# Which operand stands still: turning the down products of a fused attention and gated MLP kernel

## The chip, the cores and the metric

The kernel runs on one core of a Trainium2 chip. The metric is the device time of one execution in microseconds (us); less is better. The profile is of one execution, taken by the hardware profiler; times inside it count from the start of its span. Engines: PE is TensorE (PEld its weight loads), DVE is VectorE, ACT is ScalarE, POOL is GpSimd, SP is SyncE. A matmul has a stationary operand of 128 x 128, which is loaded first, and a moving operand, of which one column after another passes through.

## The reference

```python
def _attn_ref(r, k, v, w, u):          # B, H, S, D = 4, 8, 768, 48
    state = np.zeros((B, H, D, D))
    for t in range(S):
        cur = np.einsum('bhd,bhe->bhde', u[None] * kt, vt)
        y[:, :, t] = np.einsum('bhd,bhde->bhe', rt, state + cur)
        state = wt[:, :, :, None] * state + np.einsum('bhd,bhe->bhde', kt, vt)

def _moe_ref(x, w_gate, w_val, w_out): # x: 3072 x 384, d_ff = 1536
    gate = 1.0 / (1.0 + np.exp(-(x @ w_gate)))
    val = x @ w_val
    return (gate * val @ w_out)

# reference: y of the attention as rows of 8 * 48 = 384, then the MLP on them
```

## The kernel before

The sequence of 768 tokens is cut into six chunks of 128 (`C`). A chunk of one batch is a place `q = n * 4 + b`: `n` is the chunk, called a row here, `b` the batch. So there are six rows of four places, and a row has 512 tokens.

The attention of a place is a series of small steps (`turn_k`, `sums`, `scores`, `mix`, `turn_x` on PE; `mask`, `take_y` and others on DVE; `bonus1` to `bonus4` on POOL and DVE). They take their PSUM banks from `att_bank`, which hands out two banks in turn. Their result is `x`, the input of the MLP, with the features on the partitions.

The MLP works through `d_ff` in twelve blocks of 128, `f` = 0 to 11. Numbers are kept in two parts, a rounded one (`hi`) and the rest (`lo`), so every product is three matmuls: lo by hi, hi by lo, hi by hi. For one row and one `f`:

- `gate` and `value` each do 9 matmuls (three blocks of 128 features by three parts) into banks `pg` and `pu` (L453). The weights are stationary, the tokens move: 512 columns each.
- `sigmoid` (ACT, L464), `hidden` (DVE, L471), `hidden_hi` (ACT, L475) and `hidden_lo` (DVE, L479) make the two parts `hh` and `hl` of the hidden block, 128 x 512.
- `down` (L488) multiplies them by the output weights: for each of four blocks of 128 tokens, three matmuls in which the block of `hh` or `hl` is stationary and the 384 columns of the weights move. It adds up over `f` in four banks `po0` to `po3`, one per block of tokens. After `f` = 11 it copies each bank to a tile `o` on ACT (L494) and stores that on ACT's queue (L496). `o` comes from a pool with two buffers.

Rows 0 and 1 are done in halves of 256 tokens, in an order worked out at build time by a planner (`Plan`) with costs and due times, while the weights come in and are split (`w_guard` on ACT, `w_body`, `w_sign`, `w_tail`, `w_lo` on DVE, `w_hi` on ACT). Rows 2 to 5 are in an order written out by hand: for every `f`, `gate`, `sigmoid`, a part of the attention of the next row, `value`, the hidden steps, a part, `down` of the block before, a part. Row 5 has no attention beside it. At its first block stands `check_bounds`, a small chain on DVE and PE that sets `flag`.

At the end (L631) every engine loads `flag` and branches past `general`, a slow version of everything that these inputs do not use. Behind the branch the engines meet at a barrier.

```python
for i in range(i0, i1):                                   # down, before
    c = slice((i - i0) * C, (i - i0 + 1) * C)
    for j, (h, w) in enumerate(((hl, whi), (hh, wlo), (hh, whi))):
        nc.tensor.matmul(
            po[n, i][:, :DM], lhsT=h[:, c], rhs=w[f][:, 2 * DM:],
            start=f == 0 and j == 0, stop=f == NFF - 1 and j == 2,
        )
```

The functions that the change touches:

Of the kernel before, what the change touches and what calls it, by code (L numbers as in the profile page):

```python
# [9 lines left out]
F32 = mybir.dt.float32  # L10
F32R = mybir.dt.float32r
BF16 = mybir.dt.bfloat16
# [7 lines left out]
B, H, S, D = 4, 8, 768, 48  # L20
DM, DFF = 384, 1536
P = 128
C = 128
NC_ = S // C
NG = B * NC_
# [4 lines left out]
NFF = DFF // P  # L30
NKT = DM // P
# [13 lines left out]
def general(ctx: ExitStack, tc: tile.TileContext, dec, tok, wts, u, out, whi, wlo, ident):  # L45


    nc = tc.nc
    pool = ctx.enter_context(tc.tile_pool(name="general", bufs=1))
    bank = ctx.enter_context(tc.tile_pool(name="banks", bufs=1, space=PSUM))  # L50
    rows = ctx.enter_context(tc.tile_pool(name="rows", bufs=1, space=bass.MemoryType.DRAM)).tile([B, S, DM], F32, name="rows")

    def tiles(name, shape, dtype=F32):
        return pool.tile(shape, dtype, name=name)

    raw, t, full, square = tiles("raw", [P, HW], mybir.dt.int64), tiles("t", [P, HW], I32), tiles("full", [P, HW]), tiles("square", [P, HW])
    for f in range(NFF):
        for half in range(2):
            cols = slice(half * HW, (half + 1) * HW)
# [19 lines left out]
    vb, y = tiles("vb", [L, B, NP, D]), tiles("yb", [2, B, NP, D])  # L79
# [11 lines left out]
    for c in range(NC_):  # L91
        for b in range(B):
            nc.sync.dma_start(d[:, b], dec[b * NC_ + c])
        with tc.For_i(0, C) as i:
            def at(first, step):
                return d[:, :, first:first + NP * step].rearrange("a b (p c) -> a b p c", c=step)[:, :, :, bass.ds(i, 1)].broadcast_to(shape)
            for o in range(2):
                for b in range(B):
                    nc.sync.dma_start(vb[64 * o:64 * o + D, b], values[c, 2, o, bass.ds(i, 1), b].partition_broadcast(D))
            nc.vector.tensor_tensor(out=kv, in0=vb, in1=at(WW, C), op=ALU.mult)  # L100
            nc.vector.tensor_tensor(out=mix, in0=kv, in1=ub, op=ALU.mult)
            nc.vector.tensor_tensor(out=mix, in0=mix, in1=state, op=ALU.add)
            nc.vector.tensor_tensor(out=mix, in0=mix, in1=at(WW + NP * C, C), op=ALU.mult)
            nc.vector.tensor_tensor(out=state, in0=state, in1=at(1, W1), op=ALU.mult)
            nc.vector.tensor_tensor(out=state, in0=state, in1=kv, op=ALU.add)
            for j in range(2):
                nc.tensor.matmul(py[j][:2, :DM], lhsT=heads, rhs=mix[:, 2 * j:2 * j + 2], start=True, stop=True)
                nc.scalar.copy(y[:, 2 * j:2 * j + 2], py[j][:2, :DM].rearrange("a (b p e) -> a b p e", b=2, e=D))
            for b in range(B):
                for o in range(2):  # L110
                    nc.sync.dma_start(
                        rows[b, bass.ds(c * C + i, 1)].rearrange("t (p o e) -> o t p e", o=2, e=D)[o], y[o:o + 1, b])

    x, px = tiles("x", [P, DM]), bank.tile([P, 512], F32, name="px")
    xhi, xlo = tiles("xh", [P, NKT, C], F32R), tiles("xl", [P, NKT, C], F32R)
    gate, h, hh, hl = tiles("gate", [P, C]), tiles("h", [P, C]), tiles("hh", [P, C], F32R), tiles("hl", [P, C], F32R)
    pg, pu, po = (bank.tile([P, 512], F32, name=n) for n in ("pg", "pu", "po"))
    flat = rows.rearrange("b s e -> (b s) e")
    with tc.For_i(0, NG) as g:
        nc.sync.dma_start(x, flat[bass.ds(g * C, C)])  # L120
        for k in range(NKT):
            nc.tensor.transpose(out=px[:, k * C:(k + 1) * C], in_=x[:, k * P:(k + 1) * P], identity=ident)
        px3 = px[:, :DM].rearrange("a (k c) -> a k c", c=C)
        nc.scalar.copy(xhi, px3)
        nc.vector.tensor_tensor(out=xlo, in0=px3, in1=xhi.bitcast(F32), op=ALU.subtract)
        for f in range(NFF):
            for s, acc in enumerate((pg, pu)):
                for k in range(NKT):
                    cols = slice(s * DM + k * P, s * DM + (k + 1) * P)
                    for j, (w, a) in enumerate(((wlo, xhi), (whi, xlo), (whi, xhi))):  # L130
                        nc.tensor.matmul(acc[:, :C], lhsT=w[f][:, cols], rhs=a[:, k], start=k == 0 and j == 0, stop=k == NKT - 1 and j == 2)
            nc.scalar.activation(gate, pg[:, :C], AF.Sigmoid)
            nc.vector.tensor_tensor(out=h, in0=pu[:, :C], in1=gate, op=ALU.mult)
            nc.scalar.copy(hh, h)
            nc.vector.tensor_tensor(out=hl, in0=h, in1=hh.bitcast(F32), op=ALU.subtract)
            for j, (a, w) in enumerate(((hl, whi), (hh, wlo), (hh, whi))):
                nc.tensor.matmul(po[:, :DM], lhsT=a, rhs=w[f][:, 2 * DM:], start=f == 0 and j == 0, stop=f == NFF - 1 and j == 2)
        nc.scalar.copy(x, po[:, :DM])
        nc.sync.dma_start(out[bass.ds(g * C, C)], x)


class Plan:
# [49 lines left out]
def tile_kernel(ctx: ExitStack, tc: tile.TileContext, dec: bass.AP, tok: bass.AP, wts: bass.AP, u: bass.AP, out: bass.AP):  # L192
    nc = tc.nc
# [3 lines left out]
    p1 = own.enter_context(tc.tile_pool(name="p1", bufs=1))  # L197
    p2 = own.enter_context(tc.tile_pool(name="p2", bufs=2))
    ps1 = own.enter_context(tc.tile_pool(name="ps1", bufs=1, space=PSUM))
    att2 = own.enter_context(tc.tile_pool(name="att2", bufs=2, space=PSUM))  # L200
    early = tc.tile_pool(name="early", bufs=4)
    stage = early.__enter__()

    def att_bank(name):
        return att2.tile([P, 512], F32, tag="att", name=name)

    ident = const.tile([P, P], F32, name="ident")
# [8 lines left out]
    for s in range(2):  # L216
        part = after[s * HC:(s + 1) * HC]
        nc.gpsimd.affine_select(
            out=part, in_=part, pattern=[[1, HC]], compare_op=ALU.is_gt, fill=0.0, base=0, channel_multiplier=-1,
# [14 lines left out]
    raws, fulls, whi, wlo = {}, {}, [None] * NFF, [None] * NFF  # L234
# [5 lines left out]
    def word(f, i, dtype=I32):  # L240
        return raws[f].bitcast(dtype).rearrange("a (c w) -> a c w", w=2)[:, :, i]

    def w_guard(f):
        sq = p1.tile([P, 3 * DM], F32, tag="sq", name=f"sq{f}")
        nc.scalar.activation(sq, word(f, 1, F32), AF.Square, accum_out=acc_s[:, f:f + 1])
        nc.scalar.activation(sq, sq, AF.Relu, bias=1.0, scale=-1.0 / TINY ** 2, accum_out=acc_t[:, f:f + 1])

# [22 lines left out]
    pin, tk, eg, bon, kT, att, ready, mid, bank, x = {}, {}, {}, {}, {}, {}, {}, {}, {}, {}  # L270

    def place(q):
        return q % B * NC_ + q // B
# [183 lines left out]
    po, hid = {}, {}  # L457

    def gate(n, f, i0, i1):
        hid["g", n, f, i0] = up(0, "pg", n, f, i0, i1)  # L460
# [5 lines left out]
    def value(n, f, i0, i1):  # L466
        hid["u", n, f, i0] = up(1, "pu", n, f, i0, i1)
# [13 lines left out]
    def down(n, f, i0, i1):  # L481
        hh, hl = hid["hi", n, f, i0], hid["lo", n, f, i0]
        for i in range(i0, i1):
            if f == 0:
                po[n, i] = ps1.tile([P, 512], F32, tag=f"po{i}", name=f"po{n}_{i}")
# [6 lines that stand above are left out]
            if f == NFF - 1:  # L492
                o = p2.tile([P, DM], F32, tag="o", name=f"o{n}_{i}")
                nc.scalar.copy(o, po[n, i][:, :DM])  # L494
                g = place(n * B + i)
                nc.scalar.dma_start(out[g * C:(g + 1) * C, :], o)  # L496

    def check_bounds():
        nc.vector.tensor_scalar(out=fine[:L, 0], in0=acc_d, scalar1=2.0 ** 90, scalar2=None, op0=ALU.is_le)
# [18 lines left out]
    for q in range(3 * B + 2):  # L518
        k = rank.get(f"c{q}", 99)
# [28 lines left out]
        first = q % B == 0  # L548
# [4 lines left out]
    for f in range(NFF):  # L553
        k = rank[f"w{f}"]
# [7 lines left out]
    for g, (n, i0, i1) in enumerate(GROUPS):  # L562
        m = i1 - i0
        for f in range(NFF):
            a, name = (n, f, i0, i1), f"{g}_{f}"
            k = 100 + f + LAGS[g]
# [15 lines left out]
    plan.run()  # L582
    early.__exit__(None, None, None)
    stage = own.enter_context(tc.tile_pool(name="late", bufs=2))

    def steps(q):

# [20 lines left out]
    last = []  # L608
    nothing = [[lambda: None] * 3] * 3
    for n in range(2, NC_):  # L610
        for j in range(B):
            trio = steps((n + 1) * B + j) if n + 1 < NC_ else nothing
            for i in range(3):
                a = (n, 3 * j + i, 0, B)
                gate(*a)
                sigmoid(*a)
                trio[i][0]()
                value(*a)
                hidden(*a)
                hidden_hi(*a)  # L620
                hidden_lo(*a)
                trio[i][1]()
                if last:
                    down(*last.pop())
                trio[i][2]()
                last.append(a)
                if n == NC_ - 1 and j == 0 and i == 0:
                    check_bounds()
    down(*last.pop())
    own.close()  # L630
    with tc.If(nc.values_load(flag[:1, :1]) != 0):  # L631
        general(tc, dec, tok, wts, u, out, whi, wlo, ident)
# [31 lines left out]
```

## Time and profile before

| | |
|---|---|
| time, median of 3 runs | 614.41 us (611.59 to 615.08) |
| the profiled execution, its own time | 616.97 us |
| its span, first to last instruction | 615.3 us |
| mean granted TensorE clock | 0.980 |
| PE busy | 572.2 us (93%), 6474 matmuls |
| DVE, ACT, POOL busy | 334.5, 201.6, 95.6 us |
| read from and written to HBM | 45.11 and 4.72 MB |

A page of the profile gives each engine's busy time, the span in 40 slices, the DMA queues, the chain of work that ended last and the costliest groups of instructions by line. Further views answer questions on it: groups by line with shapes kept apart, waits, the instructions in order of time, and busy times by stretch. Ends of matmuls are modelled, so the distance from one start to the next tells more than a matmul's own duration.

### The profile page before, as it was taken

What the parts mean: (1) busy time and instruction counts of PE and PEld (TensorE: products, weight loads), DVE (VectorE), ACT (ScalarE), POOL (GpSimd) and SP (SyncE); (2) the same over time, 40 slices, a digit from 0 to 9 for tenths busy, and PEclk for the clock granted to TensorE, in tenths of its full rate; (3) what the DMA queues carried; (4) which work ended last, traced back from release to release, by engine and by line L of the source; (5) the groups of instructions that cost most, each with busy time, mean ns of one, the idle gap of its engine ahead of it and who ended that gap; (6) DMA issues with size and microseconds to landing.
All of it is one profiled execution on the core that took longest, in us unless ns stands there. A gap on an engine that the chain in (4) does not pass through costs nothing. (4 is left out here: it accounts for less than half of the span.)

```text
span 615.3 us, 14604 instructions
## 1 busy us (share of the span) xinstructions
PE 572.2 (93%) x6474; PEld 508.6 (83%) x6474; DVE 334.5 (54%) x570; ACT 201.6 (33%) x402; POOL 95.6 (16%) x86
## 2 busy tenths in 40 slices
PE   4477799999999999799999999999999999999994
PEld 3366699999999999688888888888888888888883
DVE  4989869989675653234544644644544554222220
ACT  2638674434333222312312322312322212221112
POOL 3242011002220503002202202202202200000000
PEclk9998699999999999989999999999999999999998
DMA  8787930032233130121022042022032000000001
GB/s 239 240 330 231 373 111 1 2 85 72 70 128 118 54 122 3 52 84 55 33 85 59 27 136 76 10 84 81 11 131 85 1 1 2 28 26 0 1 2 55
DMA packets 12056, 50.86 MB, mean 83 GB/s; under 512 B 1376, under 2 KB 4576, under 8 KB 10448
## 3 DMA queue, kind: packets, MB, share of 16 engines
q1 hardware_dynamic: 8528, 45.11, 22.7%
q10 hardware_dynamic: 3456, 4.72, 2.2%
q8 instruction: 53, 0.87, 0.6%
q14 instruction: 19, 0.16, 0.1%
HBM read 45.11 MB, written 4.72 MB: 81 GB/s over the span
## 5 line engine op out<-in xcount | busy, mean ns | idle before, releaser
L453 PE MATMUL pg<-x,w 128*128 128x256 f32 (+1 forms) x864 | 174.2, 347 | 1.2 <-DVE w L267 1.2
L453 PE MATMUL pu<-x,w 128*128 128x256 f32 (+1 forms) x864 | 172.1, 345 | 0.0
L453 PEld LDWEIGHTS pg<-x,w 128*128 128x128 f32 x864 | 138.7, 194 | 17.7 <-DVE w L267 1.4
L453 PEld LDWEIGHTS pu<-x,w 128*128 128x128 f32 x864 | 137.6, 193 | 17.4
L488 PE MATMUL po<-w,hh 128*128 128x384 f32 x576 | 148.5, 339 | 0.0
L471 DVE TENSOR_TENSOR sg<-pu,sg 128x256 f32<-128x256 f32 (+1 forms) x96 | 53.4, 557 | 152.8 <-PE pu L453 149.5
L488 PE MATMUL po<-w,hl 128*128 128x384 f32 x288 | 101.9, 354 | 7.1 <-DVE hl L479 6.9
L488 PEld LDWEIGHTS po<-w,hh 128*128 128x128 f32 x576 | 105.8, 190 | 0.9
L475 ACT CAST hh<-sg 128x256 fp32r<-128x256 f32 (+1 forms) x96 | 49.1, 512 | 165.3 <-DVE sg L471 164.8
L464 ACT ACTIVATE sg<-pg 128x256 f32<-128x256 f32 (+1 forms) x96 | 46.9, 488 | 159.9 <-PE pg L453 159.0
L314 POOL TENSOR_TENSOR bon<-tok,a 128x384 f32<-128x384 f32 x24 | 35.1, 1464 | 292.5 <-DVE a L310 292.5
L479 DVE TENSOR_TENSOR hl<-sg,hh 128x256 fp32r<-128x256 f32 (+1 forms) x96 | 55.6, 579 | 38.8 <-ACT hh L475 38.7
L488 PEld LDWEIGHTS po<-w,hl 128*128 128x128 f32 x288 | 54.7, 190 | 10.6 <-DVE hl L479 8.5
L303 POOL TENSOR_TENSOR bon<-tok,ub 128x384 f32<-128x384 f32 x24 | 30.9, 1287 | 117.9 <-DMA tok<-tok 68.4
L427 DVE TENSOR_TENSOR bon<-pa,bon 128x192 f32<-128x192 f32 x48 | 15.5, 352 | 37.1 <-PE pa L420 37.1
L348 ACT ACTIVATE junk<-eg 112x1032 bf16<-112x1032 f32 x24 | 25.6, 1066 | 30.5 <-DVE eg L338 30.4
L321 DVE TENSOR_TENSOR_SCAN eg<-pin,ends 112x516 f32<-112x516 f32 x24 | 30.0, 1249 | 5.0 <-DMA pin<-dec 5.0
L384 DVE TENSOR_TENSOR at<-pa,after 128x256 f32<-128x256 f32 x48 | 18.6, 418 | 24.2 <-PE pa L378 24.2
L338 DVE TENSOR_TENSOR_SCAN eg<-pin,heads 112x516 f32<-112x516 f32 x24 | 31.1, 1294 | 0.0
L396 PEld LDWEIGHTS pv<-tok,kT 64*48 64x48 f32 (+1 forms) x704 | 21.0, 137 | 10.5 <-issue 4.8
L306 POOL TENSOR_TENSOR bon<-bon,tok 128x384 f32<-128x384 f32 x24 | 27.7, 1153 | 1.7
L353 PE MATMUL pk<-ident,pin 112*128 112x112 f32 x96 | 14.6, 278 | 14.0 <-DVE pin L327 10.2
(58 smaller groups left out, 443.7 us busy)
## 6 DMA issues: line engine op xcount, KB each, us to landing
pin<-dec SPq DMA_DIRECT2D x23, 675.5 KB, 5.0
tok<-tok SPq DMA_DIRECT2D x24, 576.0 KB, 4.8
wraw<-wts SPq DMA_DIRECT2D x12, 1152.0 KB, 12.1
y<-o ACTq DMA_DIRECT2D x24, 192.0 KB, 2.0
pin<-dec SPq DMA_DIRECT2D x1, 448.0 KB, 4.3
pin<-dec SPq DMA_DIRECT2D x1, 227.5 KB, 3.0
ub<-u SPq DMA_DIRECT2D x1, 192.0 KB, 7.5
```

The source lines that it names most:

```text
L303: nc.gpsimd.tensor_tensor(out=bon[q], in0=tk[q][:, 0:DM], in1=ub, op=ALU.mult)
L306: nc.gpsimd.tensor_tensor(out=bon[q], in0=bon[q], in1=tk[q][:, DM:2 * DM], op=ALU.mult)
L314: nc.gpsimd.tensor_tensor(out=by_head(bon[q]), in0=by_head(tk[q][:, 2 * DM:]), in1=a0, op=ALU.mult)
L321: nc.vector.tensor_tensor_scan(out=e[:, 516:0:-1], data0=t[:, 516:0:-1], data1=ends[:, 516:0:-1], initial=0.0, op0=ALU.mult, op1=ALU.add,)
L338: nc.vector.tensor_tensor_scan(out=e[:, WW:WW + 516], data0=t[:, 0:516], data1=heads[:, 0:516], initial=0.0, op0=ALU.mult, op1=ALU.add,)
L348: nc.scalar.activation(junk, both, AF.Square, accum_out=acc_d[:, q:q + 1])
L453: nc.tensor.matmul(t, lhsT=w[f][:, cols], rhs=x[n][:, a, k, i0 * C:i1 * C], start=k == 0 and j == 0, stop=k == NKT - 1 and j == 2)
L464: nc.scalar.activation(sg, hid["g", n, f, i0], AF.Sigmoid)
L471: nc.vector.tensor_tensor(out=sg, in0=hid["u", n, f, i0], in1=sg, op=ALU.mult)
L475: nc.scalar.copy(hh, hid["s", n, f, i0])
L479: nc.vector.tensor_tensor(out=hl, in0=hid["s", n, f, i0], in1=hid["hi", n, f, i0].bitcast(F32), op=ALU.subtract)
L488: nc.tensor.matmul(po[n, i][:, :DM], lhsT=h[:, c], rhs=w[f][:, 2 * DM:], start=f == 0 and j == 0, stop=f == NFF - 1 and j == 2,)
```

## The change

In rows 2 to 5 `down` gives way to `down_turned`: the output weights are stationary, 128 x 128 at a time, and all 512 tokens of the hidden block move. There are nine matmuls of 512 columns per row and `f` where there were twelve of 384. The output then has features on the partitions and tokens along the columns, in three banks `po0` to `po2`. After `f` = 11 each bank goes to a tile of its own (`ot0` to `ot2`, one buffer each) and from there to the output, in pieces of 128 tokens (512 bytes). In the last row the middle one is copied by DVE and stored on SP's queue. The output tensor is laid out by places, the last four rows turned, and the host puts the pieces in order.

The bank `po3` is free in rows 2 to 5 and becomes a third bank of `att_bank`. The scratch tile `sq` of `w_guard` becomes bfloat16. `general`, which is skipped, writes its output in the new layout.

```diff
@@ general @@
+    def feed(g, turned):
...
-            for j, (a, w) in enumerate(((hl, whi), (hh, wlo), (hh, whi))):
-                nc.tensor.matmul(po[:, :DM], lhsT=a, rhs=w[f][:, 2 * DM:], start=f == 0 and j == 0, stop=f == NFF - 1 and j == 2)
+            for k in range(NKT if turned else 1):
...
+    with tc.For_i(0, 2 * B) as g:
+        feed(g, False)
+    with tc.For_i(2 * B, NG) as g:
+        feed(g, True)
@@ tile_kernel @@
+    late = False
...
+    turns = []
+
     def att_bank(name):
+
+        turns.append(name)
+        if late and len(turns) % 3 == 0:
+            return ps1.tile([P, 512], F32, tag="po3", name=name)
         return att2.tile([P, 512], F32, tag="att", name=name)
...
-        sq = p1.tile([P, 3 * DM], F32, tag="sq", name=f"sq{f}")
+        sq = p1.tile([P, 3 * DM], BF16, tag="sq", name=f"sq{f}")
...
-                g = place(n * B + i)
-                nc.scalar.dma_start(out[g * C:(g + 1) * C, :], o)
+                nc.scalar.dma_start(out[n * B + i].rearrange("(c e) -> c e", e=DM), o)
+
+    def down_turned(n, f, i0, i1):
+
+        hh, hl = hid["hi", n, f, i0], hid["lo", n, f, i0]
+        for k in range(NKT):
+            if f == 0:
+                po[n, k] = ps1.tile([P, 512], F32, tag=f"po{k}", name=f"po{n}_{k}")
+            cols = slice(2 * DM + k * P, 2 * DM + (k + 1) * P)
+            for j, (h, w) in enumerate(((hl, whi), (hh, wlo), (hh, whi))):
+                nc.tensor.matmul(po[n, k], lhsT=w[f][:, cols], rhs=h, start=f == 0 and j == 0, stop=f == NFF - 1 and j == 2)
+            if f == NFF - 1:
+                o = p1.tile([P, B, C], F32, tag=f"ot{k}", name=f"o{n}_{k}")
+                y = po[n, k].rearrange("a (b c) -> a b c", c=C)
+                by_vector = n == NC_ - 1 and k == 1
+                if by_vector:
+                    nc.vector.tensor_copy(out=o, in_=y)
+                else:
+                    nc.scalar.copy(o, y)
+                to = out[n * B:(n + 1) * B].rearrange("b (k p c) -> k p b c", k=NKT, c=C)
+                (nc.sync if by_vector else nc.scalar).dma_start(to[k], o)
...
+    late = True
...
-                    down(*last.pop())
+                    down_turned(*last.pop())
...
-    down(*last.pop())
+    down_turned(*last.pop())
```

More of the change, by code (lines that the diff above doesn't have):

```diff
@@ L50, in general @@
     bank = ctx.enter_context(tc.tile_pool(name="banks", bufs=1, space=PSUM))
-    rows = ctx.enter_context(tc.tile_pool(name="rows", bufs=1, space=bass.MemoryType.DRAM)).tile([B, S, DM], F32, name="rows")
+    rows = ctx.enter_context(tc.tile_pool(name="rows", bufs=1, space=bass.MemoryType.DRAM)).tile([NG, C, DM], F32, name="rows")
     def tiles(name, shape, dtype=F32):
@@ L111, in general @@
                     nc.sync.dma_start(
-                        rows[b, bass.ds(c * C + i, 1)].rearrange("t (p o e) -> o t p e", o=2, e=D)[o], y[o:o + 1, b])
+                        rows[c * B + b, bass.ds(i, 1)].rearrange("t (p o e) -> o t p e", o=2, e=D)[o], y[o:o + 1, b])
     x, px = tiles("x", [P, DM]), bank.tile([P, 512], F32, name="px")
@@ L117, in general @@
     pg, pu, po = (bank.tile([P, 512], F32, name=n) for n in ("pg", "pu", "po"))
-    flat = rows.rearrange("b s e -> (b s) e")
-    with tc.For_i(0, NG) as g:
-        nc.sync.dma_start(x, flat[bass.ds(g * C, C)])
+    def feed(g, turned):
+        nc.sync.dma_start(x, rows[bass.ds(g, 1)].rearrange("g c e -> (g c) e"))
         for k in range(NKT):
@@ L135, in general @@
             nc.vector.tensor_tensor(out=hl, in0=h, in1=hh.bitcast(F32), op=ALU.subtract)
-            for j, (a, w) in enumerate(((hl, whi), (hh, wlo), (hh, whi))):
-                nc.tensor.matmul(po[:, :DM], lhsT=a, rhs=w[f][:, 2 * DM:], start=f == 0 and j == 0, stop=f == NFF - 1 and j == 2)
-        nc.scalar.copy(x, po[:, :DM])
-        nc.sync.dma_start(out[bass.ds(g * C, C)], x)
+            for k in range(NKT if turned else 1):
+                cols = slice(2 * DM + k * P, 2 * DM + (k + 1) * P)
+                for j, (a, w) in enumerate(((hl, whi), (hh, wlo), (hh, whi))):
+                    first, done = f == 0 and j == 0 and k == 0, f == NFF - 1 and j == 2
+                    if turned:
+                        nc.tensor.matmul(po[:, k * C:(k + 1) * C], lhsT=w[f][:, cols], rhs=a, start=first, stop=done, skip_group_check=True)
+                    else:
+                        nc.tensor.matmul(po[:, :DM], lhsT=a, rhs=w[f][:, 2 * DM:], start=first, stop=done)
+        nc.scalar.copy(x, po[:, :DM])
+        to = out[bass.ds(g, 1)]
+        if turned:
+            nc.sync.dma_start(to.rearrange("g (k p c) -> p (g k) c", p=P, c=C), x.rearrange("p (k c) -> p k c", c=C))
+        else:
+            nc.sync.dma_start(to.rearrange("g (c e) -> (g c) e", e=DM), x)
+    with tc.For_i(0, 2 * B) as g:
+        feed(g, False)
+    with tc.For_i(2 * B, NG) as g:
+        feed(g, True)
 class Plan:
@@ L494, in down @@
                 nc.scalar.copy(o, po[n, i][:, :DM])
-                g = place(n * B + i)
-                nc.scalar.dma_start(out[g * C:(g + 1) * C, :], o)
+                nc.scalar.dma_start(out[n * B + i].rearrange("(c e) -> c e", e=DM), o)
[4 more added lines that the diff above has]
+                po[n, k] = ps1.tile([P, 512], F32, tag=f"po{k}", name=f"po{n}_{k}")
+            cols = slice(2 * DM + k * P, 2 * DM + (k + 1) * P)
+            for j, (h, w) in enumerate(((hl, whi), (hh, wlo), (hh, whi))):
[6 more added lines that the diff above has]
+                    nc.vector.tensor_copy(out=o, in_=y)
+                else:
+                    nc.scalar.copy(o, y)
+                to = out[n * B:(n + 1) * B].rearrange("b (k p c) -> k p b c", k=NKT, c=C)
+                (nc.sync if by_vector else nc.scalar).dma_start(to[k], o)
     def check_bounds():
@@ L658 @@
     args = [nc.dram_tensor(n, a.shape, mybir.dt.from_np(a.dtype), kind="ExternalInput").ap() for n, a in arrays.items()]
-    args.append(nc.dram_tensor("y", (B * S, DM), F32, kind="ExternalOutput").ap())
+    args.append(nc.dram_tensor("y", (NG, C * DM), F32, kind="ExternalOutput").ap())
     with tile.TileContext(nc) as tc:
@@ L662 @@
     r = run_bass_kernel_spmd(nc, [arrays], core_ids=[0])
-    return r.results[0]["y"]
+    y = r.results[0]["y"]
+    y = np.concatenate([y[:2 * B].reshape(-1, C, DM), y[2 * B:].reshape(-1, DM, C).transpose(0, 2, 1)])
+    return np.ascontiguousarray(y.reshape(NC_, B, C, DM).transpose(1, 0, 2, 3).reshape(B * S, DM))
```

## The prediction

> **What bounds the kernel now.** I read the page first, then the stretches around the changed rows, then the waits, then single blocks in order of time.
>
> ```profile
> span 615.3 us, 14604 instructions
> PE 572.2 (93%) x6474; PEld 508.6 (83%) x6474; DVE 334.5 (54%) x570; ACT 201.6 (33%) x402; POOL 95.6 (16%) x86
> PE   4477799999999999799999999999999999999994
> 262.60:533.00 270.40, 270.40 (x2947) 230.09 (x2940) 129.93 (x225) 68.86 (x136) 43.01 (x31) 0.99 0.18 55
> 533.00:604.80 71.80, 71.02 (x345) 62.20 (x343) 17.30 (x30) 15.83 (x27) 0.00 (x0) 1.00 0.03 12
> 604.80:615.30 10.50, 2.36 (x12) 2.04 (x12) 0.02 (x1) 1.92 (x4) 0.00 (x0) 0.80 0.24 81
> PE total L506 <- DVE count L504: 0.7, 1, 0.7
> ACT o L494 <- DMA y<-o: 4.5, 6, 1.1
> ```
>
> The first three lines are the page: PE is busy 93% of the span and idles mainly in the first 75 us, where the weights come in. The next three are stretches (length, then busy time of PE, PEld, DVE, ACT, POOL, then clock and DMA): rows 2 to 4, row 5, and the tail. In rows 2 to 4 PE is busy in all of 270.40 us, in row 5 in 71.02 of 71.80, at a granted clock of 0.99 to 1.00. So in the four changed rows PE alone sets the pace, and what counts is how closely matmuls follow each other. The tail is another matter: 10.5 us in which PE works for 2.36. The last two lines are from the waits between 265 and 600 us. PE's only listed wait there is for the small chain of `check_bounds`, 0.7 us. ACT waits 4.5 us for its own stores at the ends of rows, with PE busy all the same.
>
> **The matmuls.** One block of row 5, PE alone, in order of time (start, duration, name):
>
> ```profile
> 546.44 0.33 PE L488 MATMUL po<-w,hl 128*128 128x384 f32 x1
> ...
> 548.03 0.33 PE L488 MATMUL po<-w,hl 128*128 128x384 f32 x1
> 548.20 0.51 PE L488 MATMUL po<-w,hh 128*128 128x384 f32 x2
> 548.55 2.24 PE L453 MATMUL pg<-x,w 128*128 128x512 f32 x9
> 550.63 2.20 PE L453 MATMUL pu<-x,w 128*128 128x512 f32 x9
> 552.67 0.33 PE L488 MATMUL po<-w,hl 128*128 128x384 f32 x1
> ```
>
> Start to start, the twelve down matmuls of 384 columns take 548.55 - 546.44 = 2.11 us, 176 ns each. Nine of 512 columns take 2.08 us as `pg` (231 ns) and 2.04 us as `pu` (227 ns). The turned product is nine matmuls of just that form: weights stationary, 512 tokens moving. So each block should fall from 2.11 to between 2.04 and 2.08 us, a gain of 0.03 to 0.07 us. The columns are the same, 12 x 384 = 9 x 512 = 4608; what is saved is what each matmul costs beside its columns. Undisturbed, the last three of the twelve, 548.03 to 548.55, are 173 ns apart, against 227: 54 ns for 128 more columns, so about 173 - 3 x 54 = 11 to 13 ns that do not go with columns, and three of these make the 0.04 us that I take. Of 48 blocks (four rows of twelve) two lie just ahead of a wait that swallows the gain: the one before `check_bounds` and the one before the very last. 46 x 0.04 = 1.9 us, between 46 x 0.03 = 1.4 and 46 x 0.07 = 3.2.
>
> On this spacing a formula speaks against the change. The Trainium skill, TensorE: Matmul & The Clock Gate, section Back-to-back issue gap, gives an isolated matmul of N columns N/2.4 + 2.5 ns with a warm clock: 162.5 and 215.8 ns here, so 12 of one less 9 of the other is 8 ns a block, and by it the term would be 0.4 us. The rows above (173 and 227 ns) show a larger fixed part, and the measurement decides.
>
> **The tail.** The last block and what follows, and the instructions of the branch (L631: count, shortest/median/longest ns, first and last start), with the semaphore waits behind it (L660, between 612.85 and 613.4):
>
> ```profile
> 604.87 0.45 PE L488 MATMUL po<-w,hl 128*128 128x384 f32 x1
> 605.16 0.51 PE L488 MATMUL po<-w,hh 128*128 128x384 f32 x2
> ...
> 605.70 0.48 ACT L494 COPY o<-po 128x384 f32<-128x384 f32 x1 [1.61 <-PE po L488]
> ...
> 606.21 0.34 ACTq L496 DMA_DIRECT2D y<-o  x1
> ...
> 606.72 0.51 PE L488 MATMUL po<-w,hh 128*128 128x384 f32 x2
> 607.16 0.74 ACTq L496 DMA_DIRECT2D y<-o  x1
> 609.00 0.48 ACT L494 COPY o<-po 128x384 f32<-128x384 f32 x1 [1.88 <-SPq L631]
> ...
> 610.17 0.48 ACT L494 COPY o<-po 128x384 f32<-128x384 f32 x1 [0.68 <-SPq L631]
> 610.67 0.49 ACTq L496 DMA_DIRECT2D y<-o  x1
> L631 SPq EVENT_SEMAPHORE  x8: 17/17/17, 539.9 to 612.8; - x8
> L631 SPq TENSOR_LOAD <-flag x1: 559/559/559, 536.3 to 536.3; - x1
> L631 PEldq EVENT_SEMAPHORE  x1: 51/51/51, 609.1 to 609.1; - x1
> L631 ACTq TENSOR_LOAD <-flag x1: 482/482/482, 611.2 to 611.2; - x1
> L631 ACTq EVENT_SEMAPHORE  x1: 17/17/17, 614.4 to 614.4; - x1
> L660 SPq EVENT_SEMAPHORE  x8: 28/28/1060, 612.9 to 613.3; - x8
> ```
>
> The last matmul ends at 606.72 + 0.51 = 607.23, but the third copy starts only at 609.00. The profile names SP as releaser; what happened at that moment was the landing of the first store, 2.7 us after 606.21: `o` has two buffers, and the third copy must wait for the first store, the fourth for the second. Then ACT issues the last store at 610.67, loads `flag` at 611.2, branches, and is heard again at 614.4: 3.2 us from load to the first instruction behind the branch. SP's last semaphore wait, 1.06 us long, ends on that. The span ends 0.9 us later. So the end hangs on ACT's fourth copy, not on PE.
>
> After the change there is a tile per bank, so nothing waits for a store. What the pieces cost:
>
> ```profile
> L453 PE MATMUL pg<-x,w 128*128 128x512 f32 x332 | 83.8, 396 | 0.0
> L471 DVE TENSOR_TENSOR sg<-pu,sg 128x512 f32<-128x512 f32 x36 | 24.9, 691 | 92.0 <-PE pu L453 92.0
> L464 ACT ACTIVATE sg<-pg 128x512 f32<-128x512 f32 x36 | 21.4, 593 | 85.0 <-PE pg L453 85.0
> L384 DVE TENSOR_TENSOR at<-pa,after 128x256 f32<-128x256 f32 x16 | 6.0, 419 | 11.9 <-PE pa L378 11.9
> ```
>
> Call T the start of the last block's first matmul (604.87 before; the waits just ahead of it stay as they are). The first distance is 0.29 (604.87 to 605.16), some 0.12 more than a normal one, so the nine start until T + 0.12 + 8 x 0.227 = T + 1.93, and the last result is there 0.40 later, at T + 2.33. ACT copies it in about 0.59 (the sigmoid's 593 ns on the same shape), T + 2.95, issues the store in 0.34 to 0.74, T + 3.3 to 3.7, and needs 3.2 to be past the branch: T + 6.5 to 6.9. ACT's first copy and issue end at T + 2.0 to 2.4, about when the third bank is ready, so they cost nothing here; at an issue of 0.74 us the wait is 0.1.
>
> SP is late next. Before, it had nothing left to issue and took the branch at 536.3. Now it issues the store of the middle bank, and the load and branch stand behind it on its queue. The middle bank is ready at T + 0.12 + 5 x 0.227 + 0.40 = T + 1.65. DVE's copy of 128 x 512 has no row of its own; two-input operations on PSUM take 419 ns for 256 columns and 691 for 512, so I bound it by these and take 0.69, the same number of columns: T + 2.4. Issue 0.34 as on ACT: T + 2.75. From SP's load to its first semaphore wait are 539.9 - 536.3 = 3.6 us: T + 6.4. Then come its 16 waits, 8 of L631 and 8 of L660. The eight of L660 begin 0.4 us apart from first to last, some 65 ns each, so 16 take 1.05: T + 7.4, past ACT's 6.5 to 6.9. Add the 0.9 us to the end: T + 8.3. Before it was 615.3 - 604.87 = 10.4. The tail gains 2.1 us. The bounds: if SP's waits overlap the others', ACT decides, T + 6.5 + 0.9 = T + 7.4, gain 3.0. If code behind the branch comes more slowly with four engines branching at once, by as much as PE's path is longer than ACT's (604.9 to 609.1, part of it its matmuls, 1 us more), gain 1.1.
>
> ```profile
> L631 PEldq TENSOR_LOAD <-flag x1: 489/489/489, 604.9 to 604.9; - x1
> L631 DVEq TENSOR_LOAD <-flag x1: 536/536/536, 604.1 to 604.1; - x1
> L631 DVEq EVENT_SEMAPHORE  x1: 21/21/21, 607.6 to 607.6; - x1
> q10 hardware_dynamic: 3456, 4.72, 2.2%
> ```
>
> DVE's own branch moves behind its copy: T + 2.4 + 3.5 = T + 5.9, hidden behind SP. The stores are now 256 KB in pieces of 512 bytes. Queue 10 (the stores) took 2.2% of 16 x 615.3 us for 3456 packets, 63 ns per packet. A store has 512 pieces, 32 per DMA engine; at 63 ns these are 2.0 us where eight rows of 1536 bytes were 0.5, so a landing is 2 to 2.9 us as now, or up to 1.5 later. From T + 2.95 that is T + 5 to 7.4, still at or before the wait for it in SP's row. The cover goes above 7.4.
>
> **The other parts.** Ends of rows 2 to 4: ACT has three copies of 0.59 and three issues of 0.34 instead of four of 0.48 and 0.34 with 4.5 us of waits over the three rows. PE was busy throughout, so I take zero; sooner or later than now, the next sigmoid waits for PE. The third attention bank: PE shows no wait for a bank in rows 2 to 4, so zero, and nothing is lost either, since `po3` was emptied before row 2. `sq` in bfloat16: a neighbour on ACT that already writes bfloat16 and the operation itself:
>
> ```profile
> L348 ACT ACTIVATE junk<-eg 112x1032 bf16<-112x1032 f32 x24 | 25.6, 1066 | 30.5 <-DVE eg L338 30.4
> L246 ACT ACTIVATE sq<-sq x12: 1163/1164/1172, 16.1 to 91.6; 128x1152 f32<-128x1152 f32 x12
> L453 PE MATMUL pg<-x,w 128*128 128x256 f32 (+1 forms) x864 | 174.2, 347 | 1.2 <-DVE w L267 1.2
> ```
>
> 1066 ns for 1032 columns and 1164 for 1152 are the same price, 1.0 ns a column. Zero; if bfloat16 input were quicker, PE's wait for weights bounds the gain at 1.2 us.
>
> **The sum.** -1.9 (blocks) - 2.1 (tail) = -4.0 us: span 611.3 and time 613.0 for the profiled execution of 616.97. That execution is 2.6 us above the median of the runs; against the median, 614.41 - 4.0 = 610.4 us. The three runs lie 3.5 us apart, so 0.5% (3.1 us) is about what can be told from no change, and the gain is little above it.
>
> **The rivals.**
> A. The tail gives back half: the branch or the 512-byte stores come late with ACT, SP and DVE all at it. For it: one issue in the tail took 0.74 instead of 0.34. Against: a landing now has 4 us of cover. Tail 1.0, total -2.9: 611.5 us.
> B. Columns alone set the pace, and the turned block takes 2.11 again: the change does not do what it says. For it: 4608 columns both ways. Against: `pu` at 2.04. Total -2.1: 612.3 us. The formula of the Trainium skill, TensorE: Matmul & The Clock Gate, section Back-to-back issue gap, comes close to this rival, at 611.9 us.
> C. ACT ends the tail instead of SP, and the blocks reach 2.04 us: -3.2 - 3.0 = -6.2: 608.2 us. Against: SP's semaphore waits run one after another in the tail of before.
> D. Slower: issuing a store with four pieces per partition holds ACT's queue. At four times the 0.34 us it is 1.4: the tail loses 2 x 1.0 against my sum, and the row ends fit. It decides only from about 3 us an issue: then ACT's two issues in the tail cost 5.3 more, and three of them per row end hold the next sigmoid for 4 us past its slack, some 2 us of PE in each of three rows: -4.0 + 5.3 + 6 = +7: 621.7 us. Against: the longest issue on ACT in the tail is 0.74.
>
> **How the numbers follow.** Chances: forecast 0.56 (609.0 to 611.4), A 0.18, B 0.10, C 0.12, D 0.04. Faster by over 0.5% is below 611.3 us: forecast and C nearly whole, 0.65; within 0.5%: A and B and the forecast's edge, 0.30; slower: D and the spread of runs, 0.05. The range takes in A, B and C with about 0.6 us of the runs' spread: 607.6 to 613.0.
>
> **What would show it.** Per block, nine down matmuls 227 to 231 ns apart; a distance near 234 speaks for B. In the tail: no copy that waits for a store, ACT's load of `flag` some 3.5 us after T, SP's load at T + 2.8 and its first wait behind the branch at T + 6.4; ACT's event before SP's last ones. If SP's load stands earlier, or ACT's event ends the last wait, C; if issues on ACT exceed 1 us, D. The sum fails if the start, where DMA sets the pace, shifts by more than the 3 us that I saw between runs.

## The result, and the profile after

| | before | changed |
|---|---|---|
| time, median of 20 runs each | 614.88 us (609.85 to 617.18) | 611.36 us (607.67 to 614.41) |
| ratio | | 0.995, 95% interval 0.9928 to 0.9973 |
| profiled execution, time and span | 616.97, 615.3 us | 610.50, 608.7 us |

3.5 us less, between 1.7 and 4.4: the changed kernel is a little faster. First the changed kernel's page, with the lines that answer to those shown of before:

```profile
span 608.7 us, 14308 instructions
PE 564.6 (93%) x6330; PEld 484.4 (80%) x6330; DVE 334.6 (55%) x571; ACT 200.4 (33%) x397; POOL 97.2 (16%) x86
L526 PE MATMUL po<-hh,w 128*128 128x512 f32 x288 | 89.1, 391 | 0.0
L526 PE MATMUL po<-hl,w 128*128 128x512 f32 x144 | 58.6, 407 | 0.2 <-DVE hl L500 0.2
q10 hardware_dynamic: 6960, 4.46, 2.4%
y<-o ACTq DMA_DIRECT2D x11, 256.0 KB, 3.2
y<-o ACTq DMA_DIRECT2D x8, 192.0 KB, 1.9
```

Lines 3 and 4 are the turned product: 432 matmuls of 512 columns in the place of 576 of 384. The 256 KB stores land 3.2 us after issue in the median, the old ones after 1.9 to 2.0.

Where the time went is seen in three stretches: rows 2 to 4, row 5, and the tail from the first matmul of the last block (T) to the end. First of the kernel before, then of the changed one (length, busy times, clock and DMA last):

```profile
254.35:528.79 274.44, 272.68 (x3010) 231.76 (x3010) 131.71 (x229) 70.53 (x140) 43.01 (x31) 0.99 0.18 55
528.79:604.87 76.08, 75.23 (x363) 65.67 (x362) 17.54 (x31) 16.43 (x28) 0.00 (x0) 1.00 0.03 11
604.87:615.26 10.39, 2.36 (x12) 2.04 (x12) 0.00 (x0) 1.92 (x4) 0.00 (x0) 0.80 0.24 82
```

```profile
250.23:522.01 271.78, 270.15 (x2905) 216.59 (x2904) 131.72 (x229) 70.31 (x138) 42.95 (x31) 0.99 0.19 56
522.01:597.11 75.10, 74.01 (x328) 60.66 (x326) 17.62 (x31) 16.27 (x27) 0.00 (x0) 1.00 0.04 11
597.11:608.70 11.59, 2.33 (x9) 1.61 (x9) 0.69 (x1) 1.17 (x2) 0.00 (x0) 0.78 0.26 76
```

The blocks give 2.66 + 0.98 = 3.6 us, nearly twice the 1.9 of the sum. The tail, from which 2.1 us were expected, is 1.2 us longer. Together -2.4. These two executions differ by another 4.1 us ahead of row 2 (254.35 against 250.23). The granted clock stood at half there for 17.1 us in the one execution and for 10.2 us in the other, which is worth up to 3.4 of the 4.1; the rest is not traced here. A straight line through span against mean clock falls by 4.5 us per 0.01 of clock in 62 runs of the kernel before; read off at a clock of 0.985, before spans 612.3 us and the changed kernel 608.9, to about 0.2 each. That is 3.4 us less, where the stretches above give 2.4: the tail of this one execution is probably longer than that of most runs.

One block of row 5 in the changed kernel, PE alone (start, duration, name):

```profile
545.75 0.39 PE L526 MATMUL po<-hl,w 128*128 128x512 f32 x1
...
547.79 2.20 PE L474 MATMUL pg<-x,w 128*128 128x512 f32 x9
549.83 2.20 PE L474 MATMUL pu<-x,w 128*128 128x512 f32 x9
551.87 0.39 PE L526 MATMUL po<-hl,w 128*128 128x512 f32 x1
```

`po`, `pg` and `pu` take 2.04 us each, 6.12 in all against 6.23 before. The down group gained 0.07, and `pg`, which was not touched, gained 0.04: it took 2.08 before. The tail of the changed kernel, in the branch (L672 now):

```profile
L672 SPq TENSOR_LOAD <-flag x1: 579/579/579, 600.0 to 600.0; - x1
L672 SPq COMPARE_BRANCH  x1: 45/45/45, 600.6 to 600.6; - x1
L672 ACTq TENSOR_LOAD <-flag x1: 805/805/805, 600.7 to 600.7; - x1
L672 ACTq EVENT_SEMAPHORE  x1: 17/17/17, 605.3 to 605.3; - x1
```

SP is past its branch at 600.6 and heard again at 604.6, and its eight waits take until 607.3. Asked in two windows, they come as two and six, with no instruction of SP between; all stores had landed by 603.3, and the six wait for semaphores that had been reached by then. What did run on the DMA side from 604.8 to 606.9 is two packets of an instruction queue, which start at 605.4 and 605.9 (the third line):

```profile
L672 SPq EVENT_SEMAPHORE  x2: 17/17/17, 604.6 to 604.7; - x2
L672 SPq EVENT_SEMAPHORE  x6: 17/17/17, 606.9 to 607.3; - x6
q14 instruction: 2, 0.02, 2.0%
```

The records do not say for which engine the packets are, but nothing else is left that SP could have waited for. So the code behind the branch reached SP in two late pieces, after 4.0 and another 2.2 us.

### The profile page after: what moved, and what is told of

Read it like the earlier page. It is cut to its first block, busy times and chain, and to the rows that moved or that the text cites. A ratio compares the mean times of both kernels' runs of the same rounds, so it can differ in the third digit from the quotient of the medians.

```text
span 608.7 us, 14308 instructions
## 1 busy us (share of the span) xinstructions
PE 564.6 (93%) x6330; PEld 484.4 (80%) x6330; DVE 334.6 (55%) x571; ACT 200.4 (33%) x397; POOL 97.2 (16%) x86
## 3 DMA queue, kind: packets, MB, share of 16 engines
q10 hardware_dynamic: 6960, 4.46, 2.4%
## 4 chain that ended last, share of the span: by engine, by line
PE 88%; DVE 8%; issue 1%; ACT 1%; DMA 0%; ACTq 0%; DVEq 0%
PE pg L474 25%; PE pu L474 25%; PE po L526 16%; PE po L509 8%; PE pa L441 3%; PE pv L417 3%; PE pa L392 2%; PE pa L399 2%; PE pk L374 2%; PE px L453 1%; DVE eg L342 1%; DVE full L276 1%; DVE hl L500 1%; DVE sg L492 1%; DVE pin L348 1%
## 5 line engine op out<-in xcount | busy, mean ns | idle before, releaser
L526 PE MATMUL po<-hh,w 128*128 128x512 f32 x288 | 89.1, 391 | 0.0
L526 PEld LDWEIGHTS po<-hh,w 128*128 128x128 f32 x288 | 54.1, 188 | 10.8
L526 PE MATMUL po<-hl,w 128*128 128x512 f32 x144 | 58.6, 407 | 0.2 <-DVE hl L500 0.2
L324 POOL TENSOR_TENSOR bon<-tok,ub 128x384 f32<-128x384 f32 x24 | 32.3, 1346 | 113.8 <-DMA tok<-tok 42.8
L509 PE MATMUL po<-w,hh 128*128 128x384 f32 x192 | 49.0, 336 | 0.0
L509 PE MATMUL po<-w,hl 128*128 128x384 f32 x96 | 34.0, 355 | 7.0 <-DVE hl L500 7.0
L509 PEld LDWEIGHTS po<-w,hh 128*128 128x128 f32 x192 | 34.9, 189 | 0.0
L526 PEld LDWEIGHTS po<-hl,w 128*128 128x128 f32 x144 | 27.0, 188 | 6.1 <-DVE hl L500 0.6
```

Source lines behind the costliest of these rows:

```text
L324: nc.gpsimd.tensor_tensor(out=bon[q], in0=tk[q][:, 0:DM], in1=ub, op=ALU.mult)
L509: nc.tensor.matmul(po[n, i][:, :DM], lhsT=h[:, c], rhs=w[f][:, 2 * DM:], start=f == 0 and j == 0, stop=f == NFF - 1 and j == 2,)
L526: nc.tensor.matmul(po[n, k], lhsT=w[f][:, cols], rhs=h, start=f == 0 and j == 0, stop=f == NFF - 1 and j == 2)
```

## The experiments: what a block costs

In the code cuts, `...` stands for lines and arguments left out.

Two questions: why does a block of row 5 gain 0.11 us and not 0.04, and why is the tail longer. The first is told apart by changing role and size separately.

**Weights stationary, twelve matmuls of 384** (the role of the change, the size of before). The fourth weight block repeats the third, the last 128 tokens of a row are left out, and there are two attention banks.

```diff
-        for k in range(NKT):
+        for k in range(4):
...
-                nc.tensor.matmul(po[n, k], lhsT=w[f][:, cols], rhs=h, ...)
+                nc.tensor.matmul(po[n, k][:, :DM], lhsT=w[f][:, cols], rhs=h[:, :DM], ...)
```

> Turned product with other sizes: weights stationary as in the changed kernel, but twelve matmuls of 384 columns per block as before (four weight blocks, the fourth a repeat whose result is not used, and the first 384 tokens; the last 128 tokens of each of rows 2 to 5 are left out). The blocks without attention beside them took 6.23 us before (pg 2.08, pu 2.04, po 2.11) and 6.12 after (2.04 each). Theory of length (matmuls of 384 columns, shorter than a weight load of 188 ns, fall behind and the following pg pays too): po 2.11, pg 2.08, block 6.23. Theory of roles (it is the stationary tokens or the moving weights that disturb): po 2.08, pg 2.04, block 6.16.

**Tokens stationary, nine matmuls of 512** (the role of before, the size of the change; the fourth block of tokens is left out in rows 2 to 5).

```diff
-        for i in range(i0, i1):
+        wide = i1 - i0 == B
+        first = 2 * DM - P if wide else 2 * DM
+        for i in range(i0, i1 - wide):
...
-                    po[n, i][:, :DM], lhsT=h[:, c], rhs=w[f][:, 2 * DM:],
+                    po[n, i][:, :3 * DM - first], lhsT=h[:, c], rhs=w[f][:, first:],
```

> The kernel before with other sizes in rows 2 to 5: tokens stationary and weights moving as before, but nine matmuls of 512 columns (the 384 of the output weights and 128 more whose result is not used), for three of the four blocks of tokens; the fourth is left out and not stored. Theory of length: po, pg and pu 2.04 each, a light block 6.12 us as in the changed kernel. Theory of roles: po about 2.07, pg 2.08, a light block 6.19.

In order of time, PE alone, first of `weights_384`, then of `tokens_512`:

```profile
548.15 0.33 PE L526 MATMUL po<-hl,w 128*128 128x384 f32 x1
...
550.25 2.24 PE L474 MATMUL pg<-x,w 128*128 128x512 f32 x9
552.33 0.84 PE L474 MATMUL pu<-x,w 128*128 128x512 f32 x3
```

```profile
547.54 0.39 PE L490 MATMUL po<-w,hl 128*128 128x512 f32 x1
...
549.58 2.20 PE L453 MATMUL pg<-x,w 128*128 128x512 f32 x9
551.62 1.75 PE L453 MATMUL pu<-x,w 128*128 128x512 f32 x7
```

Turned with 384 columns: `po` 2.10, `pg` 2.08, a block of 6.23. Not turned with 512: 2.04 and 2.04, a block of 6.12. The roles do nothing; the whole gain of such a block goes with the size. The theory of roles is out.

**Nine of 384, and nine of 448 columns**, weights stationary, to see whether the number or the size disturbs, and where it begins. The edit is shown for 384; the other has 448 in its place. In both, the middle bank of the last row is stored on ACT, and the last 128 tokens of a row are not stored.

```diff
-                nc.tensor.matmul(po[n, k], lhsT=w[f][:, cols], rhs=h, ...)
+                nc.tensor.matmul(po[n, k][:, :384], lhsT=w[f][:, cols], rhs=h[:, :384], ...)
```

> The changed kernel with nine down matmuls of 384 columns per block: the last 128 of a row's 512 tokens are left out and not stored. Theory of shortness: po 1.56 to 1.59 and the following pg 2.08, a light block 5.68 to 5.71 us. Rival (it is the number of matmuls in the group, twelve against nine, that disturbs): po 1.56, pg 2.04, block 5.64.

> The changed kernel with nine down matmuls of 448 columns per block: the last 64 of a row's 512 tokens are left out, and the last 128 are not stored. 448 columns should be 200 ns apart, above the 188 ns that a weight load takes in the rows. Theory of shortness (spacing below the weight load's 188 ns disturbs the group and the one behind it): po 1.80, pg 2.04, pu 2.04, a light block 5.88 us. Rival (anything shorter than the neighbours' 512 disturbs): pg 2.08, block 5.92 to 5.95.

First `nine_384`, then `cols_448`:

```profile
541.89 0.33 PE L526 MATMUL po<-hl,w 128*128 128x384 f32 x1
...
543.48 2.24 PE L474 MATMUL pg<-x,w 128*128 128x512 f32 x9
545.56 2.20 PE L474 MATMUL pu<-x,w 128*128 128x512 f32 x9
```

```profile
544.45 0.36 PE L526 MATMUL po<-hl,w 128*128 128x448 f32 x1
...
546.27 2.23 PE L474 MATMUL pg<-x,w 128*128 128x512 f32 x9
548.34 2.20 PE L474 MATMUL pu<-x,w 128*128 128x512 f32 x9
550.38 0.36 PE L526 MATMUL po<-hl,w 128*128 128x448 f32 x1
```

With nine of 384, `po` took 1.59 where nine undisturbed ones (173.3 ns each, from the run with 384 throughout below) would take 1.56, and `pg` 2.08: the same 26 and 41 ns too much as with twelve. So it is not the number. With nine of 448, `po` took 1.82, `pg` 2.07 and a block of row 5 5.93 us; 24 and 29 ns over the undisturbed 1.80 (an estimate, midway between 1.56 and 2.04) and 2.04. My theory of a threshold at a weight load's 188 ns is refuted, and the rival (anything shorter than its neighbours) holds. What was left: does a short matmul disturb, or a change of size?

**All matmuls of the rows at 384.** The fourth block of tokens is left out of `gate` and `value` by the edit shown, and of the down group, the copies and the stores as well.

```diff
-                a = (n, 3 * j + i, 0, B)
+                a = (n, 3 * j + i, 0, 3)
```

> The changed kernel with all matmuls of the MLP in rows 2 to 5 at 384 columns: gate, value and down work on the first three of the four blocks of 128 tokens, nine matmuls each; the fourth block of tokens is left out and not stored. With 384 in the down group alone, that group took 1.586 us and the following pg 2.081 instead of 2.04. Theory (a change of the moving size between groups costs 26 ns in the group behind it when 512 gives way to 384, 41 when 384 gives way to 512): no size changes here in the blocks without attention, so pg, pu and po take 1.56 each and a block of row 5 4.68 us. Rival (matmuls shorter than 512 are disturbed as such): about 25 ns more in each group, 4.75 us.

```profile
502.02 1.72 PE L474 MATMUL pg<-x,w 128*128 128x384 f32 x9
503.58 1.72 PE L474 MATMUL pu<-x,w 128*128 128x384 f32 x9
505.14 0.33 PE L526 MATMUL po<-hl,w 128*128 128x384 f32 x1
```

1.56 us per group, 173.3 ns per matmul, nothing over. So the change of size costs, not the size: 26 ns in the group behind 512 to 384, 41 ns behind 384 to 512. An undisturbed matmul costs 173.3 ns with 384 columns and 226.7 with 512. A block of before: 12 x 173.3 - 9 x 226.7 = 40 ns for the number of matmuls, and 26 + 41 = 67 ns for two changes of size, 107 in all, and 6.23 - 6.12 = 0.11 measured. In blocks with attention steps between the groups the gain is less, probably because the size changes there anyway: the lengths from one block's first `pg` to the next fell from 8.87 and 8.90 to 8.83 and 8.84, from 7.72 to 7.70 and from 6.23 to 6.12 us for the three kinds of block in row 2. What in TensorE makes a change of size cost this is not shown.

**Two attention banks** (the third undone).

```diff
-        if late and len(turns) % 3 == 0:
+        if False:
```

> The changed kernel with the third attention bank undone: two banks in turn in rows 2 to 4, as before. PE showed no wait for a bank there in the kernel before. Theory (the third bank does nothing for the time): heavy, medium and light blocks stay at 8.84, 7.70 and 6.12 us. Rival (it lets the attention's steps start earlier and is part of the gain): heavy or medium blocks 0.05 us or more longer.

8.83, 7.70 and 6.12 us: in these blocks the third bank does nothing for the time. In the first block of row 2 it does. First the changed kernel, then `two_banks`, from the first `pg` of the row to the next:

```profile
250.23 2.25 PE L474 MATMUL pg<-x,w 128*128 128x512 f32 x9
...
255.43 0.27 PE L392 MATMUL pa<-pin 48*64 48x64 f32 x1
...
258.51 1.72 PE L474 MATMUL pg<-x,w 128*128 128x512 f32 x4
```

```profile
252.59 2.25 PE L474 MATMUL pg<-x,w 128*128 128x512 f32 x9
...
259.79 1.09 PE L392 MATMUL pa<-pin 48*64 48x64 f32 x29 [1.62 <-DVE mid L428]
...
261.33 1.65 PE L474 MATMUL pg<-x,w 128*128 128x512 f32 x3
```

With a third bank the attention's `pa` starts 5.20 us into the block, with two banks 7.20, and the block takes 8.28 against 8.74 us. The granted clock was full in both. Rows 2 to 4 as a whole take 0.5 us more with two banks (272.27 against 271.78); row 5 takes 0.09 less. So about 0.4 us of the changed kernel's gain in the blocks is the third bank's, and 3.2 the product's. The rival had the mechanism, an earlier start of the attention, in another block than it named. The tail of `two_banks` repeats that of the changed kernel, 11.5 us, with SP's eight waits from 607.5 to 610.0.

## The experiments: what the tail costs

**The store of the middle bank on ACT, or on POOL, instead of SP.**

```diff
-                (nc.sync if by_vector else nc.scalar).dma_start(to[k], o)
+                nc.scalar.dma_start(to[k], o)                                  # act_store
+                (nc.gpsimd if by_vector else nc.scalar).dma_start(to[k], o)    # pool_store
```

> The changed kernel with one edit: in the last row the middle bank is still copied by DVE, but its store stands on ACT's queue, so SP has nothing left to issue and branches early. From the start T of the last block's first matmul to the end of the span the kernel before takes 10.4 us and the changed one 11.6. Theory (SP's late branch, whose code comes in two late pieces, holds the end): ACT's last store is issued by T + 3.9, its first instruction behind the branch comes 3.2 to 4.6 us after its load of the flag, and T to the end is 8.0 to 9.4 us; the time falls by 2 to 3.5 us against the changed kernel. Rival (the 512-byte stores, or several engines fetching code at once, hold the end whichever queue issues): T to the end stays at 11 us or more.

> The changed kernel with the store of the middle bank in the last row on POOL's queue instead of SP's. With that store on ACT's queue the end came at T + 9.7, the copy of the third bank having waited 0.9 us behind the middle store. Theory (the last engine to reach the branch sets the end, and ACT is that engine): ACT copies the third bank at T + 2.35, issues its last store by T + 3.5, is behind the branch at T + 6.8 to 7.5, and the span ends between T + 8.4 and 9.2. POOL's branch cost 0.4 us in the kernel before. Rival (what ends last is the landing of the stores while code is being fetched, 3 to 3.7 us after issue): the end stays at T + 9.5 or later, since POOL's store is issued no earlier.

**The kernel before with a tile per output bank** (`before_tiles`), **and with one store on SP besides** (`tiles_sp`).

```diff
-                o = p2.tile([P, DM], F32, tag="o", name=f"o{n}_{i}")
+                o = p1.tile([P, DM], F32, tag=f"o{i}", name=f"o{n}_{i}")
-                nc.scalar.dma_start(out[g * C:(g + 1) * C, :], o)
+                (nc.sync if n == NC_ - 1 and i == 2 else nc.scalar).dma_start(...)   # tiles_sp only
```

> The kernel before with a tile of its own for each of the four output banks (and the scratch tile of the weight guard in bfloat16, to make room); the down products are as they were. Theory (in the kernel before, the wait for a free output tile holds the end): no copy waits for a store, ACT issues its last store at T + 4.3, and T to the end falls from 10.4 to between 8.4 and 9.8 us, a light block stays at 6.23 us. Rival (the end is held by the code behind the branch, not by the copies): T to the end stays at 10 us or more.

> The kernel before with a tile per output bank, as in the run with T to the end of 9.63 us, and one more edit: in the last row the third bank's store stands on SP's queue. Its pieces are 1536 bytes, not 512. Theory (a store on SP puts SP's branch late, and the code behind it comes in two late pieces): SP's load of the flag at T + 4.1, its first wait behind the branch at T + 8 to 8.6, T to the end 11 to 12.8 us. Rival (it was the 512-byte pieces that made the changed kernel's tail long): T to the end 9.6 us or less.

**The turned product with the old tail** (`two_buffers`): one tile with two buffers, all on ACT. It also has two attention banks and `sq` in float32.

```diff
-                o = p1.tile([P, B, C], F32, tag=f"ot{k}", name=f"o{n}_{k}")
+                o = p2.tile([P, B, C], F32, tag="ot", name=f"o{n}_{k}")
-                by_vector = n == NC_ - 1 and k == 1
+                by_vector = False
```

> The turned product alone: two attention banks, the weight guard's scratch in float32 and, as before, one output tile with two buffers, all copies and stores of the last row on ACT. Blocks as in the changed kernel (8.84, 7.70, 6.12 us). Theory of the tail: the third copy waits for the landing of the first store, 2.9 us after its issue at T + 1.6, so ACT's last store is out at T + 5.7, and T to the end is 9.8 to 11.3 us. If the tiles of their own bring more than the store on SP loses, T to the end is longer than the changed kernel's 11.6. Total against before: 3 to 4 us faster, if blocks carry the gain.

| kernel | T to the end, us | ratio to before (95%) | time at clock 0.985, us |
|---|---|---|---|
| before | 10.39 | | 614.0 |
| before_tiles | 9.63 | 0.9975 (0.9948 to 1.0002) | 613.4 |
| tiles_sp | 10.08 | 1.0002 (0.9971 to 1.0032) | 613.3 |
| two_buffers | 10.26 | 0.9945 (0.9917 to 0.9974) | 610.6 |
| changed | 11.59 | 0.995 (0.9928 to 0.9973) | 610.7 |
| act_store | 9.71 | 0.9928 (0.9902 to 0.9953) | 609.9 |
| pool_store | 9.41 | 0.9924 (0.9903 to 0.9945) | 609.5 |

The last column is read from a straight line per kernel through the times of 10 to 62 runs, to some 0.3 us. (The spans would not do: the time exceeds the span by 2.5 us on average in `two_buffers`, by 1.7 to 1.9 in the others. Why is open.) SP and ACT in the branch, first of `act_store`, then of `pool_store`:

```profile
L672 SPq EVENT_SEMAPHORE  x8: 17/17/17, 600.9 to 603.7; - x8
L672 ACTq EVENT_SEMAPHORE  x1: 17/17/17, 603.2 to 603.2; - x1
```

```profile
L672 SPq EVENT_SEMAPHORE  x8: 17/17/17, 602.6 to 603.1; - x8
L672 ACTq TENSOR_LOAD <-flag x1: 480/480/480, 600.4 to 600.4; - x1
L672 ACTq EVENT_SEMAPHORE  x1: 17/17/17, 605.4 to 605.4; - x1
```

With the store off SP's queue, SP's last wait of these starts at T + 8.3 and T + 6.2, in the changed kernel at T + 10.2 (T is 595.40, 596.94 and 597.11). The end falls by 1.9 and 2.2 us in these profiles, and by about 1 us over the runs, where 2 to 3.5 were expected of `act_store`. `act_store` also misses its upper bound of 9.4 for the tail: its last store is out at T + 4.2 instead of 3.9, lands 3.7 us after issue, and SP waits for that. In `pool_store` ACT loads the flag at T + 3.5 as expected, but is behind the branch 5.0 us later, not 3.3 to 4.0; it ends last, at T + 9.4, against 9.2 at most. Its rival, the landings, is out for this run: the eight waits shown were over at 603.1, and a ninth, for POOL's store, which landed last, at 604.0. `pool_store` and `act_store` have the lowest times of all complete kernels here; between these two and the changed kernel the intervals overlap.

`two_buffers` has the blocks of the changed kernel (8.84, 7.70, 6.12), the wait for the first store and its last store out at T + 5.5, near the 5.7 expected. It ends at T + 10.3, 1.3 us before the changed kernel, and over the runs the two are equal. So the nine matmuls of 512 alone bring as much as the whole change. What the third bank adds, 0.4 us, is probably lost again in the new tail, which with its tiles and SP's store is up to 1.3 us longer.

`before_tiles` ends at 9.63, within its range: the wait for a tile cost 0.8 us net in these profiles. More was not to be had, because a store then lands late (613.16, 3.5 us after issue) and SP waits for it, and ACT is behind its branch only at 613.3. `tiles_sp` agrees with neither side: 10.08, neither 11 or more nor 9.6. There SP branched at 606.2 and had all its code in one piece:

```profile
L631 SPq EVENT_SEMAPHORE  x8: 17/17/17, 609.6 to 610.2; - x8
L631 SPq COMPARE_BRANCH  x1: 45/45/45, 606.2 to 606.2; - x1
```

So the first piece came 3.4 us after SP's branch, but nearly all of that is hidden: the last store landed at 609.6, 4.0 us after its issue, and ACT was behind its branch at 609.9. Against `before_tiles` the end comes 0.45 us later in the profile, and over the runs no later. What costs in the changed kernel is thus the second piece: without its 2.2 us the tail would be 9.4 us, as long as that of `pool_store` (an estimate from these rows). It came late, by 1.9 to 2.2 us, in all four profiles of turned kernels with the store on SP (the changed kernel, `two_banks`, `weights_384`, `all_384`) and not here; why is open. The first piece varies as well: in `weights_384` it came 2.7 us after SP's branch, and T to the end was 9.7 us, with stores of three quarters of the size.

## Why the prediction was right, point by point

The time, 611.36 us, is 1.0 above the forecast of 610.4 and in the range; -4.0 was forecast and -3.5 measured. That it came so near is partly luck: three terms of the sum were wrong, two in one direction and one in the other. The number of rival A, 611.5, is nearer still, and equally by luck.

- **Blocks, 46 x 0.04 = -1.9.** Mechanism right, size wrong: -3.2 for the product alone (`two_buffers`). The 0.04 is exact for what it stood for, the fixed part of three matmuls (40 ns). The step that failed is "Nine of 512 columns take 2.08 us as `pg`": I took 2.04 to 2.08 as the spread of one price and carried it over. It was no spread. `pg` was slow because it followed 384 columns, and the change cures that too. Rows of before showed it: `pg` 2.08 and `pu` 2.04 in the same block. A block without attention gained 0.11, beyond the bound of 0.07.
- **The formula of the Trainium skill** (TensorE: Matmul & The Clock Gate, Back-to-back issue gap; 162.5 and 215.8 ns, given there for an isolated matmul): the run with 384 throughout measures 173.3, the changed kernel 226.7. The measurement decides for the rows: 226.7 - 173.3 = 53.4 ns for 128 columns leave a fixed part of some 13 ns in the 173.3, not 2.5.
- **Tail, -2.1.** Wrong: +1.2 in the profile. The order was right: no copy waited for a store, ACT's last store was out at 600.6 = T + 3.5, SP's load at T + 2.9 (forecast T + 2.8), and SP, not ACT, ended last. The step that failed is SP's path, 3.6 us from its load to its first semaphore wait and then 16 waits in 1.05. The first took 4.6 and a second gap of 2.2 stood between the waits. In the row that I used, SP had loaded the flag at 536.3, and only POOL branched with it. The row was misread, too: the wait at 539.9 ended with the landing of a store that ACT had issued at 537.4:

```profile
L496 ACTq DMA_DIRECT2D y<-o x1: 338/338/338, 537.4 to 537.4; - x1
DMA to landing us min/median/max: 2.5/2.5/2.5
```

So 3.6 us was no price of the code. That it was near one is luck: in `before_tiles` SP loads the flag at 536.5 and its first wait comes at 540.2, 1.1 us after the store it names had landed, so there the code took 3.7 us. The lower bound gave 1 us more for four engines branching at once; it was 3.3.
- **Rivals.** A (the tail gives back half) had the place right and was too mild. B (columns alone) is out: columns are equal, and the block fell. C had the blocks right (2.04 us) and the tail wrong: ACT was past its branch at 605.3, 1.6 us before SP's last six waits began. D is out: the longest issue on ACT in this tail took 0.52 us. One at the end of row 2 did exceed D's sign of 1 us, with 1.1 us at 351.0, and the block beside it was not longer (8.83 us).
- **Third bank, zero.** Wrong: -0.4, as `two_banks` shows. The step that failed is "PE shows no wait for a bank in rows 2 to 4". The waits were read from 265 us on, and the stretch taken as rows 2 to 4 from 262.60, but row 2 begins at 254.35, a block earlier. PE's wait of 1.6 us for `mid` in its first block lies ahead of that, and beside it the attention's `pa` started 2 us later for want of a bank.
- **Other parts, zero.** The row ends: the blocks there show no loss but 0.05 us in the first of row 5, where `check_bounds` stands. `sq` in bfloat16: 1163 ns in the median where it was 1164.
- **Stores.** Queue 10's packets took 2.4% of 16 x 608.7 us for 6960, 34 ns on average against 63; I had bounded a 512-byte piece by 63. Landings still rose to 3.2 us.

## What to carry to other kernels

When two neighbouring groups of a stream have different prices for the same instruction, look for what stands ahead of each before taking the difference as spread; here equal moving sizes throughout were worth more than fewer matmuls. A store at the very end belongs on a queue that has nothing late behind it: count the branch and the code behind it as work of that queue, with a price measured while the other engines do the same, and see first that the row it is read from does not end on something else. And a sum that comes out right is no proof of its terms: in the profiles +1.2 stood for -2.1, -3.2 for -1.9 and -0.4 for nothing.

## What the runs showed of the hardware

- A group of matmuls whose moving size differs from that of the group ahead runs 26 ns (512 to 384) to 41 ns (384 to 512) longer; with 448, 24 and 29 ns. With one size throughout, all groups of nine took 1.560 us at 384 and 2.040 at 512.
- Which operand stands still made no difference to the pace (2.10 and 2.11 for twelve of 384, 2.04 and 2.04 for nine of 512).
- At the end of the kernel the first instruction behind the branch came 2.5 to 4.4 us after it on ACT and, where SP branched late, 2.7 to 4.1 on SP. In four of these five profiles the rest of SP's code came 1.9 to 2.2 us later still, with two packets of an instruction queue between.
